# Batch 1's q and k loaded by four heads, early constant products and a new order of steps in a fused attention and gMLP kernel

## The chip, the cores and the metric

The kernel runs on one core of one Trainium2 chip. The metric is the device time of one execution in microseconds. The kernel before took 168.78 us, the median of three runs (167.84 to 169.89).

## What is computed

Two blocks follow each other: sliding-window attention with four sink positions, and a gMLP block on its output. Cut to what matters:

```python
# attention: batch 4, 8 heads, 768 positions, head size 64; n_sink 4, window 128
scores = (q @ k.transpose(0, 1, 3, 2)) / 8
keep = (pos[None, :] < 4) | ((rel >= 0) & (rel < 128))      # rel = row - column
a = softmax(where(keep, scores, -1e9))
x = (a @ v)                       # heads side by side: (4, 768, 512)
# gMLP: d_model 512, d_ff 1024
h = gelu_tanh(x @ w_in)           # (4, 768, 1024)
u, v = h[..., :512], h[..., 512:]
v_n = (v - mean(v)) / sqrt(var(v) + 1e-6) * g_ln
v_s = einsum('ts,bsd->btd', w_sg, v_n) + b_sg[None, :, None]
out = x + (u * v_s) @ w_out
```

All inputs and the output are float32 in HBM; the products are computed in bfloat16.

## The kernel before

The kernel is one long list of steps, STEPS (line 20). Each word of it names a function and its indices, and a loop at the end (line 615) calls them in this order. Inside an engine the order of the list is the order of execution; engines, and the two DMA queues (the software queue, issued by POOL, and SyncE's, SP), run past each other as far as semaphores between producer and consumer allow. Nothing else plans the work: what stands behind a waiting instruction on its engine waits too.

Indices: b is the batch (0 to 3), p a pair of heads (0 to 3), g a pair of 128-row blocks (0 to 2), t or j a block of 128 rows (0 to 5), hf a half of the 768 rows, dc a block of 128 of the 512 gate columns. A last letter names the engine: D is VectorE (DVE), A is ScalarE (ACT), P is GpSimd (POOL).

The steps of a batch, in the order of its data:

- LQ, LK (line 219, 222; the load itself is `load`, line 210) bring q and k as bfloat16 through the software queue; LFQ (line 225) brings the first four blocks of batch 0's q as float32 through SP; LV and LVH (line 231, 241) bring v. LW, LWS, LWO (line 246 to 255) bring the two halves of w_in, the two halves of w_sg and w_out, all through the software queue. LC and LG (line 258, 262) bring the sink rows of v, g_ln and b_sg (the tile b_bc) through SP.
- q and k are needed with the head dimension on the partitions. HOW (line 15) gives the way for each batch: "B" turns a loaded block with TensorE (TQ, TK through `turns`, line 320; eight transposes of 128 columns into one PSUM tile for two row blocks), and EQ, EK (`turned`, line 364) copy the result out of PSUM; "C" turns by a DMA transpose on SP (DQ, DK, `by_dma`). FTQ and FEQ do the same for LFQ's blocks.
- QK (line 428) makes the scores of a head pair and row pair, EX (line 441) takes their exponent on ACT into a tile P, MK (line 445) sets what lies outside the window to zero, on DVE by a product with a mask or on POOL by two affine selects. Where a QK step carries a last index 1, the mask is added on TensorE instead, by a product with a bias tile. KS, SK and SX do the sink columns.
- AV (line 467) multiplies P with v, NR (line 491) divides by the sum into x_sb. XT and XE (or the DMA transpose XD) turn x.
- MV and GV make the gate half of h (TensorE, then gelu on ACT), BN, RS, NM its mean and variance, Z the normalised half. MU and GU make the other half, already turned. WT and WE turn w_sg once, in batch 0. SP (a step, line 579) is the product with w_sg, GT and GM (line 586, 591) add b_sg and multiply with u, GM on DVE or POOL; OU (line 595) is the product with w_out, RA (line 602) adds x, ST stores.

PSUM holds two rings: two score tiles (sc) for QK, MV and MU, and four smaller ones (mm) for all else. A step that takes a tile waits until the step that read it last is done. k16, q16, kT and qT have two tiles each, so batch 2 takes those of batch 0.

HM n (line 179) asks that the next step that takes a PSUM tile first runs n products of constants into it (`fresh`, line 182), which its own products then overwrite. The list before has no HM.

Of the kernel before, what the change touches and what calls it, by code (L numbers as in the profile page):

```python
# [9 lines left out]
BF16 = mybir.dt.bfloat16  # L10
# [1 line left out]
ALU = mybir.AluOpType  # L12

PARTS = (0,)
HOW = "BBCC"
VHOW = "THHH"
BIG = 1e9


STEPS = """  # L20
LFQ.0 LK.0.0 LFQ.1 LFQ.2 LK.0.1 LFQ.3 LK.0.2 IDEN LK.0.3 IDEN2 FTQ.0 FILL LQ.0.4 FEQ.0.A FTQ.1 LQ.0.5 LC FTQ.2 MASK
FEQ.1.A LK.0.4 MASK0 TK.0.0 LK.0.5 FTQ.3 EK.0.0.A ZERO LG LV.0.0 QK.0.0.0 KS.0 FEQ.2.D QK.0.1.0.1 EX.0.0.0 LV.0.1
EX.0.1.0 TK.0.1 LV.0.2 QK.0.2.0 FEQ.3.A QK.0.3.0.1 VSK EX.0.2.0 LV.0.3 VSO EK.0.1.D TQ.0.2 EX.0.3.0 MK.0.0.0.D LV.0.4
QK.0.0.1 EQ.0.2.D QK.0.1.1 EX.0.0.1 LV.0.5 VSM.0 TK.0.2 EX.0.1.1 MK.0.2.0.D LW.0 QK.0.2.1.1 EK.0.2.D MK.0.0.1.P
QK.0.3.1.1 EX.0.2.1 SK.0.1 EX.0.3.1 LK.1.0 MK.0.1.1.D QK.0.0.2 AV.0.0.0 AV.0.1.0 LWS.0 AV.0.2.0 NR.0.0.0 SX.0.1
QK.0.1.2.1 EX.0.0.2 NR.0.1.0 LW.1 SK.0.2 NR.0.2.0 EX.0.1.2 AV.0.3.0 AV.0.0.1 MK.0.0.2.P NR.0.3.0 AV.0.1.1 SX.0.2
NR.0.0.1 QK.0.2.2 QK.0.3.2 LK.1.1 EX.0.2.2 NR.0.1.1 AV.0.2.1 AV.0.3.1 NR.0.2.1 AV.0.0.2 EX.0.3.2 MK.0.2.2.P XT.0.0
NR.0.3.1 AV.0.1.2 NR.0.0.2 XE.0.0.A XT.0.1 LQ.1.0 MK.0.3.2.D AV.0.2.2 XE.0.1.A NR.0.1.2 LQ.1.1 AV.0.3.2 MV.0.0
NR.0.2.2 LQ.1.2 NR.0.3.2 LWS.1 XT.0.2 GV.0.0 LK.1.2 MV.0.1 XE.0.2.D BN.0.0 LK.1.3 LQ.1.3 WT.0 GV.0.1 MV.0.2 LQ.2.0
BN.0.1 LQ.2.1 WT.1 GV.0.2 WT.2 LQ.1.4 MU.0.0 BN.0.2 RS.0.1 LQ.1.5 TQ.1.0 GU.0.0 MU.0.1 RS.0.2 WE.0.A WE.1.D WE.2.D  # L30
LK.1.4 NM.0.1 NM.0.2 Z.0.0.D Z.0.1.A MU.0.2 Z.0.4.D LK.2.0 GU.0.1 EQ.1.0.D LK.2.1 Z.0.2.A Z.0.3.D Z.0.5.D TK.1.0
LK.1.5 GU.0.2 SP.0.0.0 EK.1.0.D LVH.1.0 QK.1.0.0 GT.0.0.0 QK.1.1.0 WT.3 TQ.1.1 EX.1.0.0 WE.3.D LVH.1.1 SP.0.0.1 VSM.1
EX.1.1.0 EQ.1.1.D WT.4 DQ.2.0 LK.2.2 QK.1.2.0 KS.1 WE.4.A GT.0.0.1 QK.1.3.0 TK.1.1 MK.1.0.0.D LK.2.3 EX.1.2.0 WT.5
EK.1.1.D SP.0.0.2 EX.1.3.0 LWO WE.5.A QK.1.0.1 LK.2.4 GT.0.0.2 QK.1.1.1 TQ.1.2 EX.1.0.1 MK.1.1.0.D LQ.2.2 SP.0.1.0
EQ.1.2.D EX.1.1.1 MK.1.3.0.D LQ.2.3 DK.2.0 SK.1.0 MK.1.0.1.D QK.1.2.1 SX.1.0 LQ.2.4 QK.1.3.1 GM.0.0.0.D TK.1.2
# [39 lines left out]
def kernel(  # L75
# [14 lines left out]
    nc = tc.nc  # L90
# [16 lines left out]
    sb = ctx.enter_context(tc.tile_pool(name="sb", bufs=1))  # L107
# [22 lines left out]
    mm_ring = Ring("mm", 4, [128, 512], F32, psum)  # L130
# [21 lines left out]
    c16 = Ring("c16", 6, [128, d_model], BF16)  # L152
    iden = sb.tile([128, 128], BF16, name="iden")
    iden32 = sb.tile([128, 128], F32, name="iden32")
    mask0 = sb.tile([128, 512], BF16, name="mask0")
    mask1 = sb.tile([128, 512], BF16, name="mask1")
    bias0 = sb.tile([128, 512], BF16, name="bias0")
    bias1 = sb.tile([128, 512], BF16, name="bias1")
# [23 lines left out]
    def fresh(ring, key):  # L182
        t = ring.new(key)
        for _ in range(pre[0]):
            nc.tensor.matmul(t if ring is mm_ring else t[:, 0, :], iden, bias1, start=True, stop=True)
        pre[0] = 0
        return t

# [18 lines left out]
    def plain(ring, b, t):  # L207
        return ring.get((b, t // 3)).bitcast(F32)[:, d_model * (t % 3):d_model * (t % 3 + 1)]

    def load(ring, src, b, i):  # L210
        if HOW[b] in "FD":
            return nc.sync.dma_start(out=plain(ring, b, i).rearrange("p (h d) -> p h d", h=H), in_=heads(src, b, i))
        if HOW[b] == "A":
            dst = ring.get(b)[:, NH * HP * i:NH * HP * (i + 1)].rearrange("p (h f) -> p h f", h=HP)
# [49 lines left out]
        return nc.sync.dma_start(out=b_bc, in_=moe_b_sg.partition_broadcast(128))  # L264

    def IDEN():
        make_identity(nc, iden32)
# [385 lines left out]
```

## Time and profile before

| | before |
|---|---|
| median of three runs | 168.78 us |
| the profiled execution's own time | 168.27 us |
| its span, first to last instruction | 166.5 us |
| busy: ACT, POOL | 96.7, 105.8 us |
| HBM read, written | 24.81 MB, 6.29 MB |
| issues of q, k loads by POOL | 44, 0.91 to 0.93 us each |

PE is TensorE's products, PEld its weight loads. Engines work beside each other, so shares do not add up to one; what counts in a stretch is the engine, queue or wait that ends last there. The share of a DMA queue is the time that its packets took, summed over 16 engines; packets of one engine overlap, so it can be above 100%. A time line row gives start, length, engine, line, operation, the tiles written and read, and, in brackets, how long the engine was idle before and what ended it. The time to landing is counted from the issue's start.

### The profile page before, as it was taken

The numbers are of one execution on the slowest core, as the hardware profiler recorded it, in microseconds if no ns is written. First come the engines' busy times: TensorE is split into PE (matmuls) and PEld (weight loads), VectorE is DVE, ScalarE is ACT, GpSimd is POOL, SyncE is SP. The second block draws the span as 40 slices with busy tenths as digits, with TensorE's granted clock in tenths as the row PEclk, the third lists the DMA queues.
The fourth block names the chain that finished last, engine by engine and source line by source line (L and its number), as shares of the span: only waits on it lengthen the run. The fifth ranks groups of instructions, "written<-read, shape, count | busy, mean of one in ns | idle before, by whom it ended". The sixth has DMA issues, their size and how long they took to land.

```text
span 166.5 us, 3659 instructions
## 1 busy us (share of the span) xinstructions
PE 146.5 (88%) x1448; PEld 94.2 (57%) x1458; DVE 123.1 (74%) x289; ACT 96.7 (58%) x107; POOL 105.8 (64%) x131
## 2 busy tenths in 40 slices
PE   0598899997799767979999999999999999899990
PEld 0455467595566445744666675458656744585540
DVE  0346487775859999756976989859989964885881
ACT  3249789468659464297799660856988003683000
POOL 7997969599996399997807994907025930034220
PEclk9999999999789999999999999999999999999999
DMA  5999999999999999999999988999900436510055
GB/s 117 172 165 200 126 174 206 171 189 158 148 132 140 166 177 160 111 158 161 149 107 154 128 251 204 180 186 206 209 32 0 88 74 217 192 69 0 0 193 186
DMA packets 100321, 24.39 MB, mean 146 GB/s; under 512 B 94800, under 2 KB 97104, under 8 KB 100304
## 3 DMA queue, kind: packets, MB, share of 16 engines
q0 software_dynamic: 72912, 11.67, 102.4%
q1 hardware_dynamic: 27392, 12.49, 37.3%
q8 instruction: 11, 0.18, 0.4%
q14 instruction: 6, 0.05, 0.1%
HBM read 24.81 MB, written 6.29 MB: 187 GB/s over the span
## 4 chain that ended last, share of the span: by engine, by line
PE 43%; DVE 19%; DMA 12%; POOL 10%; ACT 7%; issue 6%; another core or an unknown queue 0%; ACTq 0%; DVEq 0%; POOLq 0%
PE mm L599 12%; PE mm L582 11%; DMA w_in_sb<-in_moe_w_in_dram 7%; PE sc L521 6%; PE sc L562 5%; DMA k<-in_k_dram 5%; DVE gtmp L587 4%; DVE P L450 4%; POOL q L217 4%; PE sc L438 3%; POOL k L217 3%; DVE wsg_gated L592 2%; ACT vt L525 2%; DVE x_sb L496 2%; DVE st L534 2%
## 5 line engine op out<-in xcount | busy, mean ns | idle before, releaser
L443 ACT ACTIVATE P<-sc 128x1024 bf16<-128x1024 f32 (+1 forms) x48 | 43.2, 956 | 14.6 <-PE sc L438 14.5
L582 PE MATMUL mm<-wsgT,z 128*128 128x384 bf16 x192 | 35.8, 333 | 3.8 <-DVE z L555 1.5
L582 PEld LDWEIGHTS <-z 128*128 128x128 bf16 x192 | 18.1, 99 | 16.3 <-issue 3.6
L592 POOL TENSOR_TENSOR wsg_gated<-gtmp,uT 128x384 bf16<-128x384 bf16 x18 | 16.9, 949 | 14.7 <-DVE gtmp L587 11.0
L587 DVE SCALAR_TENSOR_TENSOR gtmp<-mm,g_sb,b_bc 128x384 bf16<-128x384 f32 x32 | 19.2, 611 | 6.1 <-PE mm L582 6.0
L521 PE MATMUL sc<-w_in_sb,xT 128*128 128x512 bf16 x92 | 21.9, 379 | 2.0 <-ACT xT L194 1.0
L534 DVE BATCH_NORM_STATS2 st<-vt 128x6 f32<-128x512 f32 x24 | 15.4, 684 | 10.7 <-ACT vt L525 10.7
L217 POOL DMA_DIRECT2D k<-in_k_dram x24 | 22.2, 931 | 1.1 <-POOLq L636 0.8
L599 PE MATMUL mm<-w_out_sb,wsg_gated 128*128 128x512 bf16 x91 | 21.8, 379 | 0.3
L217 POOL DMA_DIRECT2D q<-in_q_dram x20 | 18.0, 909 | 6.4 <-PE sc L438 2.8
L562 PE MATMUL sc<-xT,w_in_sb 128*128 128x256 bf16 x192 | 21.9, 273 | 0.0
L562 PEld LDWEIGHTS <-w_in_sb 128*128 128x128 bf16 x192 | 18.6, 98 | 2.8
L496 DVE TENSOR_TENSOR x_sb<-mm,rcp 128x384 bf16<-128x384 f32 (+1 forms) x36 | 18.5, 513 | 1.2
L450 DVE TENSOR_TENSOR P<-P,mask 128x768 bf16<-128x768 bf16 (+1 forms) x26 | 18.8, 731 | 0.6 <-ACT P L443 0.6
L543 POOL TENSOR_TENSOR rs<-rs,neg_half 128x4 f32<-128x4 f32 (+1 forms) x8 | 7.3, 913 | 18.6 <-DVE rs L538 17.9
L453 POOL TENSOR_SCALAR_AFFINE_SELECT P<-P 128x512 bf16<-128x512 bf16 x17 | 11.5, 678 | 10.8 <-ACT P L443 10.7
L603 DVE TENSOR_TENSOR ot<-mm,x_sb 128x512 f32<-128x512 f32 x24 | 15.8, 684 | 3.4 <-PE mm L599 3.4
L479 PE MATMUL mm<-v_sb,P 128*128 128x65 bf16 x192 | 16.6, 194 | 1.2 <-DVE gtmp L587 0.8
L438 PE MATMUL sc<-qT,kT 64*128 64x128 bf16 (+1 forms) x256 | 15.4, 241 | 1.1 <-ACT P L443 0.6
L525 ACT ACTIVATE vt<-sc 128x1024 f32<-128x1024 f32 x12 | 12.2, 1024 | 7.0 <-PE sc L521 6.1
L521 PEld LDWEIGHTS <-xT 128*128 128x128 bf16 x96 | 9.1, 98 | 12.5 <-ACT xT L194 1.3
L483 PE MATMUL mm<-v_sb,P 128*128 128x65 bf16 x160 | 15.7, 194 | 0.4 <-POOL P L456 0.4
(75 smaller groups left out, 226.8 us busy)
## 6 DMA issues: line engine op xcount, KB each, us to landing
out_dram<-ot SPq DMA_DIRECT2D x24, 256.0 KB, 3.0
k<-in_k_dram POOLq DMA_DIRECT2D x24, 128.0 KB, 7.3
q<-in_q_dram POOLq DMA_DIRECT2D x20, 128.0 KB, 8.3
v_sb<-in_v_dram POOLq DMA_DIRECT2D x6, 384.0 KB, 9.5
wsg_gated<-in_moe_w_sg_dram POOLq DMA_DIRECT2D x2, 576.0 KB, 10.6
ot<-in_q_dram SPq DMA_DIRECT2D x4, 256.0 KB, 5.1
w_in_sb<-in_moe_w_in_dram POOLq DMA_DIRECT2D x2, 512.0 KB, 11.2
v_sb<-in_v_dram POOLq DMA_DIRECT2D x6, 128.0 KB, 9.5
```

Of the source, the lines that this page charges most:

```text
L217: return nc.gpsimd.dma_start(out=dst.rearrange("p (h d) -> p h d", h=H), in_=heads(src, b, i))
L438: nc.tensor.matmul(sc[:, hl, c:c + 128 * ni], at(kT, b)[rows, j, p, :], at(qT, b)[rows, i:i + ni, p, :], start=not biased, stop=(not biase ...
L443: nc.scalar.activation(out=P.new((b, p, g))[:, :, 0:w], in_=sc_ring[b, p, g][:, :, 0:w], func=AF.Exp, scale=scale)
L450: nc.vector.tensor_mul(pt[:, :, 0:w], pt[:, :, 0:w], m.unsqueeze(1).to_broadcast([128, 2, w]))
L496: nc.vector.tensor_mul(x_sb.get(b)[:, i0:i0 + n, 128 * p:128 * (p + 1)].rearrange("p t (h d) -> p t h d", h=2), av[:, :, :, 0:Dh], rcp[:, ...
L521: nc.tensor.matmul(hp[:, jl, :], xT[b][:, 2 * g + jl, c, :], w_in_sb[:, c, d_half:2 * d_half], start=(c == 0), stop=(c == KD - 1))
L534: nc.vector.bn_stats(out=sts[jl], in_=vt[b, g][:, jl, :])
L562: nc.tensor.matmul(hp[:, dc // 2, 256 * (dc % 2):256 * (dc % 2 + 1)], w_in_sb[:, c, 128 * dc:128 * (dc + 1)], xT[b][:, 2 * g:2 * g + 2, c, :],
L582: nc.tensor.matmul(ps[:, 0:NH], z[b][:, si, 128 * dc:128 * (dc + 1)], wsgT[:, si, NH * hf:NH * (hf + 1)], start=(si == 0), stop=(si == NT ...
L587: nc.vector.scalar_tensor_tensor(out=gtmp.new((b, hf, dc)), in0=mm_ring["g", b, hf, dc][:, 0:NH], scalar=g_sb[:, dc:dc + 1], in1=b_bc[:, N ...
L592: (nc.vector if e == "D" else nc.gpsimd).tensor_mul(gated(b, hf)[:, dc, :], gtmp[b, hf, dc], uT[b][:, dc, NH * hf:NH * (hf + 1)])
L599: nc.tensor.matmul(ps, gated(b, hf)[:, dc, 128 * tl:128 * (tl + 1)], w_out_sb[:, dc, :], start=(dc == 0), stop=(dc == KU - 1))
```

## The change

Four things change. HOW becomes "BACC": batch 1's q and k are loaded in the way "A", which is in the code of both kernels: a load takes four heads with all 768 rows, partition p gets rows 6p to 6p + 5 of each head, a run of 1.5 KB in HBM in place of 256 bytes, and there are four such loads (LQ.1.0, LQ.1.1, LK.1.0, LK.1.1) in place of twelve. TQ.1 and TK.1 then turn a pair of heads g (0 to 3) with all its rows, by twelve transposes of 64 columns, two side by side in the partitions of one PSUM tile; EQ.1 and EK.1 copy 768 columns out and put the rows back in order, reading PSUM with a stride. A tile `warm` of zeros is set by DVE in the first step (WARM), the constant products read it in place of iden and bias1, and three HM steps ask for 6 + 2 + 2 of them. And the whole list of steps is in a new order, with other engines for some of them: XE four times on DVE for ACT, WE twice; MK on POOL 23 times for 17; GM on POOL 12 times for 18.

```diff
-HOW = "BBCC"
+HOW = "BACC"
 STEPS = """
-LFQ.0 LK.0.0 LFQ.1 LFQ.2 LK.0.1 LFQ.3 LK.0.2 IDEN LK.0.3 IDEN2 FTQ.0 FILL LQ.0.4 FEQ.0.A FTQ.1 LQ.0.5 LC FTQ.2 MASK
...
+WARM LFQ.0 IDEN LFQ.1 LK.0.0 LFQ.2 IDEN2 FILL LFQ.3 LK.0.1 LK.0.2 HM.6 FTQ.0 LC LK.0.3 FTQ.1 MASK LQ.0.4 MASK0 HM.2
+FTQ.2 VSK LQ.0.5 VSO FEQ.0.D FEQ.1.A FTQ.3 FEQ.2.A LK.0.4 TK.0.0 FEQ.3.A LK.0.5 EK.0.0.D LV.0.0 ZERO HM.2 QK.0.0.0
+QK.0.1.0.1 EX.0.0.0 LV.0.1 VSM.0 TK.0.1 EX.0.1.0 LV.0.2 QK.0.2.0 EK.0.1.D EX.0.2.0 QK.0.3.0.1 KS.0 LV.0.3 MK.0.0.0.D
+TQ.0.2 EX.0.3.0 MK.0.2.0.D QK.0.0.1 LQ.1.0 EQ.0.2.D EX.0.0.1 QK.0.1.1.1 LV.0.4 SK.0.1 EX.0.1.1 TK.0.2 LV.0.5
+QK.0.2.1.1 EK.0.2.D SX.0.1 MK.0.0.1.P AV.0.0.0 EX.0.2.1 AV.0.1.0 AV.0.2.0 NR.0.0.0 QK.0.3.1.1 LW.0 NR.0.1.0 SK.0.2
+EX.0.3.1 NR.0.2.0 LK.1.0 QK.0.0.2 AV.0.3.0 AV.0.0.1 LK.1.1 NR.0.3.0 SX.0.2 AV.0.1.1 EX.0.0.2 AV.0.2.1 NR.0.0.1
+QK.0.1.2 NR.0.1.1 XT.0.0 MK.0.0.2.P EX.0.1.2 AV.0.3.1 XE.0.0.D QK.0.2.2 QK.0.3.2 NR.0.2.1 MK.0.1.2.P EX.0.2.2 TQ.1.0
+NR.0.3.1 AV.0.0.2 EQ.1.0.A MK.0.2.2.P TQ.1.1 NR.0.0.2 EX.0.3.2 XT.0.1 AV.0.1.2 LK.2.0 XE.0.1.A AV.0.2.2 MK.0.3.2.D
+MV.0.0 LK.2.1 EQ.1.1.D LW.1 NR.0.1.2 AV.0.3.2 NR.0.2.2 LWS.0 GV.0.0 MV.0.1 NR.0.3.2 LWS.1 BN.0.0 LQ.1.1 XT.0.2 GV.0.1
+LQ.2.0 TK.1.0 XE.0.2.D TK.1.1 LQ.2.1 EK.1.0.D TK.1.2 DK.2.0 TK.1.3 LK.2.2 BN.0.1 QK.1.0.0 MV.0.2 EX.1.0.0 LG EK.1.1.D
+RS.0.1 MU.0.0 GV.0.2 LQ.2.2 NM.0.1 Z.0.0.A Z.0.1.D LQ.2.3 BN.0.2 MU.0.1 GU.0.0 LVH.1.0 EK.1.2.D EK.1.3.A WT.0 GU.0.1
+WT.1 WE.0.D MU.0.2 RS.0.2 WE.1.D Z.0.2.A NM.0.2 Z.0.4.A Z.0.5.D KS.1 LK.2.3 MK.1.0.0.D WT.2 GU.0.2 WT.3 WE.2.D WT.4
+WT.5 WE.3.D WE.4.A QK.1.1.0 WE.5.D QK.1.0.1 LVH.1.1 TQ.1.2 Z.0.3.D TQ.1.3 EQ.1.2.D SP.0.0.0 EX.1.1.0 LWO DQ.2.0
...
+GM.0.0.3.P QK.1.3.2 EX.1.3.1 SP.0.1.2 NR.1.0.1 MK.1.2.2.P MK.1.3.0.D EX.1.3.2 SP.0.1.3 NR.1.1.0 MK.1.3.1.P
+GT.0.1.2 QK.2.0.0 QK.2.1.0 EX.2.0.0 GT.0.1.3 AV.1.2.0 MK.1.3.2.P AV.1.3.0 EX.2.1.0 AV.1.1.1 MK.2.0.0.D NR.1.2.0
+AV.1.2.1 GM.0.1.2.P QK.2.2.0 NR.1.3.0 QK.2.3.0 EX.2.2.0 LK.2.4 AV.1.3.1 NR.1.1.1 OU.0.0 EX.2.3.0 LQ.3.0 NR.1.2.1
+XT.1.0 LVH.2.0 NR.1.3.1 QK.2.0.1 DQ.2.2 QK.2.1.1 EX.2.0.1 XE.1.0.D OU.0.1 RA.0.0 LK.3.0 EX.2.1.1 XT.1.1 GM.0.1.3.D
+XT.1.2 GM.0.1.1.D LK.2.5 MV.1.0 RA.0.1 LVH.2.1 KS.2 XE.1.1.D XE.1.2.D MV.1.1 GV.1.0 MK.2.1.1.P BN.1.0 LQ.3.1 MV.1.2
...
+MK.3.1.2.P SP.2.0.2 GT.2.0.0 GT.2.0.1 AV.3.1.1 GM.2.0.0.D GT.2.0.2 GM.2.0.1.P AV.3.2.1
+NR.3.1.1 AV.3.3.1 OU.2.3 NR.3.2.1 NR.3.3.1 OU.2.4 RA.2.3 XD.3.1 OU.2.5 RA.2.4 SP.2.0.3 GM.2.0.2.D ST.2.3 ST.2.4 MV.3.0
+GT.2.0.3 GM.2.0.3.D OU.2.0 GV.3.0 OU.2.1 RA.2.0 MV.3.1 ST.2.0 RA.2.1 RA.2.5 ST.2.1 BN.3.0 ST.2.5 MV.3.2 ST.1.5 GV.3.1
+BN.3.1 OU.2.2 GV.3.2 MU.3.2 BN.3.2 RS.3.1 MU.3.0 GU.3.2 RA.2.2 RS.3.2 NM.3.1 NM.3.2 Z.3.0.A Z.3.1.D MU.3.1 Z.3.2.D
...
+    warm = sb.tile([128, 512], BF16, name="warm")
...
-            nc.tensor.matmul(t if ring is mm_ring else t[:, 0, :], iden, bias1, start=True, stop=True)
+            nc.tensor.matmul(t if ring is mm_ring else t[:, 0, :], warm[:, 0:128], warm, start=True, stop=True)
...
+    def WARM():
+        nc.vector.memset(warm, 0.0)
```

In the list before, three LK.0 loads stand ahead of IDEN, LG (with b_sg) stands ahead of LV.0.0, LK.1.0 is the only load of batch 1 or 2 ahead of w_in's second half (LW.1), half of w_sg (LWS.0) stands ahead of it, and WT.3 to WT.5, TQ.1.1 to TK.1.2 and all of QK.1 stand behind SP.0.0.0.

## The prediction

> **What bounds the kernel now.** I read the page first, then busy time by stretches, then the waits and the time line inside the stretch that loses most. Page and stretches (columns: stretch, length, then busy time of PE, PEld, DVE, ACT and POOL with instruction counts, granted clock, DMA share, GB/s):
>
> ```profile
> PE 146.5 (88%) x1448; PEld 94.2 (57%) x1458; DVE 123.1 (74%) x289; ACT 96.7 (58%) x107; POOL 105.8 (64%) x131
> q0 software_dynamic: 72912, 11.67, 102.4%
> ```
>
> ```profile
> 0.00:27.00 27.00, 19.08 (x247) 13.11 (x249) 13.86 (x49) 16.42 (x21) 23.16 (x37) 1.00 1.96 162
> 27.00:40.20 13.20, 12.97 (x120) 9.47 (x118) 8.41 (x26) 8.65 (x10) 10.84 (x13) 1.00 1.83 180
> 40.20:67.80 27.60, 22.43 (x285) 14.82 (x286) 24.70 (x44) 17.59 (x21) 23.15 (x29) 0.94 2.10 154
> 67.80:106.50 38.70, 37.41 (x369) 23.04 (x371) 31.12 (x74) 27.68 (x30) 29.20 (x34) 1.00 1.59 158
> 106.50:137.80 31.30, 30.71 (x294) 19.68 (x296) 26.55 (x61) 16.94 (x18) 13.95 (x16) 1.00 0.89 121
> 137.80:163.20 25.40, 23.90 (x145) 14.09 (x144) 18.40 (x41) 9.43 (x10) 5.46 (x6) 1.00 0.32 117
> ```
>
> The cuts are at first products: MV.0.0, SP.0.0.0, MV.1.0, MV.2.0, MV.3.0. From 67.8 on PE is the bound (37.4 of 38.7, 30.7 of 31.3, 23.9 of 25.4). In 40.2 to 67.8 it is not: DVE is busy 24.7 of 27.6. Up to 40 the loads decide: w_in's first half is issued at 16.64 and lands 9.9 later, at 26.5, and MV.0.0 starts at 27.1. The software queue delivers in the order of issue and always owes something: its small q loads, issued 0.87 apart, land 0.84 apart.
>
> DVE is not slow by its own work only. In the time line:
>
> ```profile
> 59.04 2.60 DVE L592 TENSOR_TENSOR wsg_gated<-gtmp,uT 128x384 bf16<-128x384 bf16 x1
> 59.62 0.63 POOL L453 TENSOR_SCALAR_AFFINE_SELECT P<-P 128x512 bf16<-128x512 bf16 x1
> 60.21 0.63 POOL L456 TENSOR_SCALAR_AFFINE_SELECT P<-P 128x512 bf16<-128x512 bf16 x1
> 60.80 0.63 POOL L453 TENSOR_SCALAR_AFFINE_SELECT P<-P 128x512 bf16<-128x512 bf16 x1
> ```
>
> That product has a median of 0.357 us; it stood still for 2.2 us while POOL ran selects back to back.
>
> The last stage has one hole:
>
> ```profile
> 140.00 1.28 ACT L525 ACT_TABLE_LOAD   x1 [10.83 <-PE sc L521]
> 142.37 1.89 PE L521 MATMUL sc<-w_in_sb,xT 128*128 128x512 bf16 x8 [0.72 <-ACT vt L525]
> ```
>
> MV.3.2 waits for a score buffer that GV.3.0 holds, which waits for its table: some 1.2 us with nothing between.
>
> **Prices, from unstalled rows.** PE: MV 1.73 (eight products, 29.27 to 31.00), MU 1.74 (33.73 to 35.48), SP 0.98 (eight in 7.80 at the end), OU 0.87, eight transposes 0.44 (35.48 to 35.92), WT 0.35, QK 0.16 or 0.21, AV 0.36 to 0.6. DVE: GT 0.60, GM 0.36, NR 0.18 + 0.56, MK 0.55 or 0.68, RA 0.69, BN 1.5 to 1.7, WE 0.55, XE 0.69, Z 0.54. Multiplied with the counts of both lists of steps, PE has 134 us either way, DVE 125 either way. POOL loses 61 − 53 issues (−8 small ones at 0.92 = −7 us), gets six mask pairs more (23 for 17, 1.27 each) and six gate products fewer (12 for 18, 0.95): −5 us in all. ACT loses four XE and two WE, wins two Z, and has two table loads more (12 for 10).
>
> **The parts.**
>
> Loads. Twelve loads of 256 KB read become four of 786 KB. Small ones take 0.84 us of queue, so 10.1. No row has this shape; by bytes, half of w_sg (1.18 MB read in 3 KB runs) takes 2.8, so 786 KB takes 1.9. Ends: w_in's first half at its fastest (1.05 MB in 1.75) gives 1.3; no gain at all gives 2.5. I take 1.9 as the nearest row: 7.6 in place of 10.1.
>
> Order of that queue. Moved past it: LQ.1.0 now stands ahead of LV.0.4, LK.1.0, LK.1.1, LK.2.0, LK.2.1 ahead of w_in's second half, and that ahead of both halves of w_sg. Before, LV.0.5 landed at 14.79 + 10.0 = 24.8. After it lands at about 26.0: one big load ahead (+1.9), against which b_bc (384 KB, in flight 9.4 to 16.2) is gone from this time (−0.7). Then w_in 27.8 (+1.75), LK.1.0 and LK.1.1 31.6, two small 33.3, LW.1 35.9 (+2.6; it was 20.39 + 12.4 = 32.8), LWS.0 38.7, LWS.1 41.6 (39.0 before), LQ.1.1 43.5. The weights come some 3 us later. PE's order puts work there: from MV.0.0 to SP.0.0.0 it has 15.8 us (MV 5.2, MU 5.2, six WT 2.1, six turns 2.0, rest 1.3) against 12.7. So MV.0.0 at 27.8, MU.0.0 about 36, SP.0.0.0 at 44.0 instead of 40.25, with 103.2 us of PE work left instead of 106.5. Up to here it is a draw, and there is no cover: each microsecond of a later weight is one of PE's.
>
> Turns. Ninety-six transposes of 64 columns for forty-eight of 128. The trace has products into 32 columns (L417): four of 512 columns take 0.40 us together, one takes 0.389, so column groups overlap. By that row twelve turns take 0.33, serially 0.64 (12 × 0.44/8): 0 to +2.5 us in all; I take 0.5. The copies out read PSUM with a stride: 768 elements take 0.55 by WE's row, or 0.95 at the rate of the f32 copy (512 in 0.69). I take 0.95; two of them, +0.8, fall into the stretch where DVE is full.
>
> The Trainium skill, TensorEngine Tiling (Array Packing), Restrictions and Gotchas, speaks against this part: column tiling excludes the fast weight load, and changing the mode drains the array. The trace's 32-column loads take 92 ns and the full ones 98, so it shows no loss there; by the rule the turns would cost the serial end, 2 us more.
>
> Warm products. The memset of warm (row of mask: 0.49) ends at about 1.3; six products of 512 columns, at twice the warm pitch of 0.22, end by 4.0, and the first q block lands at about 4.1. The identity is made before the first k load and not after three, which takes away the 4.8 us that PE waits for it, and puts 0.5 us ahead of LK.0.0. TK.0.0 needs LK.0.1, so QK.0.0.0 stays at 11.3. Faster products (the bias pair 0.82 at 11.71, 0.50 at 13.91) gain 0.5 us there; then w_in's landing takes it all back. Worth nothing; without the cover at most 1 us either way.
>
> The stretch from SP.0.0.0 to MV.1.0. PE has 17.8 us in both. DVE had 20.7 by prices and was held 4 more; after it has 18.5 + 0.4, since the EK, WE and most EQ are already done, and I leave 3 us for standing behind POOL (the clock, granted at 0.94 here, I leave as it is). 44.0 + 22 = 66.0 for MV.1.0 instead of 67.9, though OU.0.0, OU.0.1 and two XT more are already done.
>
> From MV.1.0. PE has 85.3 us left instead of 88.7. Stage by stage, with the losses of before: to SP.1.0.0 14.5 + 1.6 gives 82; to MV.2.0 DVE leads, 16.9 + 1, gives 100; to MV.3.0 29.0 + 1.7. Here a new wait comes: between AV.2.3.1 and MV.2.1 PE now has 5.3 us (three OU, four QK, SK, MV.2.0) where it had 7.9, while NR.2.3.1 ends 2.5 us after the AV and XD took 4.7 to land: 7.2 − 5.3 = 1.9 late. That gives 132.6. To the end 26.0 + 0.8 (the hole before MV.3.2 now holds OU.2.0 to OU.2.2; OU.2.3 to OU.2.5, SP.2.0.3 and MV.3.0 cover XD.3.1) gives 159.4. The span ended 3.3 us after the last DVE step, and the execution is 168.27 against a span of 166.5, 1.8 around it: 159.4 + 3.3 + 1.8 = **164.5**. The median of the runs is 168.78, 0.5 above the profiled one; I leave that as scatter.
>
> **Rivals.**
>
> Weights late (**167.5**, chance 0.16). If a four-head load takes 2.5, three of them stand ahead of LWS.1: +1.8 at SP.0.0.0; LWO, behind the same queue, then holds OU.0.0, ahead of XT.1.0, for another microsecond: 164.5 + 3. For it: the chain of before already has w_in's DMA with 7%. Against: runs of 2 and 3 KB move faster in the same queue.
>
> POOL's selects hold DVE (**172**, chance 0.24), the one that ends slower. Six pairs more stand on POOL, three in a row twice, and DVE has twenty gate products for fourteen, all between PE and the gated buffers that OU needs. If each of six runs costs the 2.2 us of the row above, DVE loses 13 where I left 5: 164.5 + 8. It decides beyond four such stalls. Against: masks on DVE fall from 26 to 20. The Trainium skill, SBUF — State Buffer, SBUF: two separate sides, calls this an exclusive lock held for one instruction; by that each stall would be one select, 0.63, and this rival would vanish; the row shows four.
>
> The parts don't do what they say (**165.5**, chance 0.12): the turns run serially, +2, half of it before SP.0.0.0 where PE has just enough time, half where it waits for copies anyway.
>
> My forecast has 0.48. Faster by over 1%: 0.48 + 0.12 = 0.60, same 0.16, slower 0.24; 1% is about what a measurement of this kernel tells from no change. The range goes from 160 (three loads at 1.3 ahead of LWS.1, −1.8; copies at 0.55, −0.8; no wait at MV.2.1, −1.9) to 172.
>
> **What would show it.** LWS.1 landing near 41.6 and LQ.1 loads 1.9 us apart; SP.0.0.0 near 44; MV.1.0 near 66; a PE wait before MV.2.1 of some 2 us; no hole before MV.3.2; L592 on DVE with few instances above 1 us. Wrong if PE waits for a DMA anywhere between 28 and 44 us for more than 2 us, or if the stretch from SP.0.0.0 to MV.1.0 is again near 27 us.

## The result, and the profile after

The changed kernel takes **170.63 us** (median of 20 runs, 169.10 to 173.77), the kernel before 168.43 on the same chip (20 runs, 167.07 to 170.65). The ratio is 1.012, with a 95% interval of 1.009 to 1.015: slower by over 1%, where I had forecast 164.5 and a gain. The time lies inside my range of 160 to 172, on the wrong side.

The profile taken with the result is of a disturbed execution (span 172.1), so the lines below are of a second profile of the same kernel, "again" (171.23 us, span 169.5). From its page, busy time and the software queue:

```profile
PE 150.9 (89%) x1516; PEld 96.4 (57%) x1516; DVE 131.3 (77%) x295; ACT 96.8 (57%) x106; POOL 99.2 (59%) x129
q0 software_dynamic: 62544, 11.67, 87.7%
```

The change does to the queue what it says: 10,400 packets fewer for the same 11.67 MB, and 87.7% in place of 102.4%. Yet PE is busy 4.4 us longer. The stretches, cut at the same first products as before (MV.0.0, SP.0.0.0, MV.1.0, MV.2.0, MV.3.0), tell where:

```profile
0.00:29.09 29.09, 23.65 (x274) 15.19 (x275) 15.64 (x52) 16.37 (x20) 25.46 (x41) 0.89 1.59 159
29.09:46.84 17.75, 16.91 (x218) 12.56 (x215) 14.76 (x36) 15.43 (x18) 10.52 (x12) 0.98 1.42 180
46.84:74.77 27.93, 21.79 (x269) 14.42 (x266) 22.69 (x40) 15.09 (x18) 22.75 (x28) 0.88 2.07 136
74.77:108.61 33.84, 32.50 (x333) 19.99 (x331) 30.41 (x66) 25.37 (x28) 23.16 (x30) 1.00 1.39 151
108.61:139.02 30.41, 29.70 (x279) 19.02 (x278) 26.46 (x59) 15.78 (x17) 13.80 (x17) 1.00 0.95 127
139.02:164.90 25.88, 25.88 (x158) 15.26 (x156) 20.36 (x46) 8.72 (x9) 3.53 (x4) 1.00 0.38 105
```

The third stretch was to shrink from 27.6 to 22 us and is 27.9, with DVE no longer its bound (22.7 of 27.9) and the clock at 0.88. The waits of "again" between 50 and 70 us name the cause (columns: sum, times, longest):

```profile
PEld L483 <- DMA v_sb<-in_v_dram: 5.6, 2, 4.8
PE mm L483 <- DMA v_sb<-in_v_dram: 5.0, 2, 4.5
```

PE's time line there, POOL's at the issue of that load, and PE in the stretches behind the wait:

```profile
61.37 0.51 PE L442 MATMUL sc<-qT,kT 64*128 64x256 bf16 x8
66.40 0.35 PE L483 MATMUL mm<-v_sb,P 128*128 128x65 bf16 x3 [4.53 <-DMA v_sb<-in_v_dram]
```

```profile
46.29 1.42 POOL L243 DMA_DIRECT2D v_sb<-in_v_dram  x1 [1.95 <-DMA q<-in_q_dram]
```

```profile
66.00:68.00 2.00, 1.60 (x27) 1.60 (x28) 0.69 (x3) 0.00 (x0) 2.00 (x3) 0.50 1.12 58
68.00:70.00 2.00, 2.00 (x33) 1.80 (x32) 1.57 (x6) 0.00 (x0) 2.00 (x3) 0.50 1.86 139
70.00:72.00 2.00, 2.00 (x28) 1.23 (x25) 1.32 (x4) 1.54 (x2) 1.64 (x2) 0.85 2.62 151
72.00:75.00 3.00, 3.00 (x42) 2.22 (x41) 2.48 (x7) 1.95 (x3) 0.00 (x0) 1.00 2.45 159
```

AV.1.2.0 is the first product that reads heads 4 to 7 of v of batch 1, and their load, LVH.1.1, lands at 66.4. It was issued only at 46.29, because POOL first waited 1.95 us for a q load (LQ.1.1, landed at 46.0). While it waited, eight transfers of this queue were in flight, LQ.1.1 the oldest. From issue to landing it took 20.1 us. PE stood still for 4.8 us, and for 4 us behind that it was busy at half its clock. Where before PE waited for DVE, it now waits for a load.

### The profile page after: what moved, and what is told of

It reads as the page before. It is cut to its first block, busy times and chain, and to the rows that moved or that the text cites. A ratio compares the mean times of both kernels' runs of the same rounds, so it can differ in the third digit from the quotient of the medians.

```text
span 172.1 us, 3783 instructions
## 1 busy us (share of the span) xinstructions
PE 150.1 (87%) x1503; PEld 95.3 (55%) x1516; DVE 131.3 (76%) x295; ACT 97.0 (56%) x106; POOL 99.2 (58%) x129
## 3 DMA queue, kind: packets, MB, share of 16 engines
q0 software_dynamic: 62544, 11.67, 85.4%
## 4 chain that ended last, share of the span: by engine, by line
PE 45%; DMA 28%; DVE 12%; POOL 4%; ACT 4%; issue 3%; SPq 1%; DVEq 0%; ACTq 0%
DMA v_sb<-in_v_dram 12%; PE mm L586 10%; PE mm L603 9%; DMA q<-in_q_dram 9%; PE sc L525 8%; DMA ot<-in_q_dram 5%; PE sc L566 4%; PE sc L442 4%; DMA out_dram<-ot 2%; DVE P L454 2%; DVE st L538 2%; PE mm L483 2%; DVE wsg_gated L596 2%; DVE gtmp L591 2%; DVE ot L607 1%
## 5 line engine op out<-in xcount | busy, mean ns | idle before, releaser
L447 ACT ACTIVATE P<-sc 128x1024 bf16<-128x1024 f32 (+1 forms) x48 | 43.8, 953 | 24.0 <-PE sc L442 22.8
L586 PE MATMUL mm<-wsgT,z 128*128 128x384 bf16 x192 | 34.1, 327 | 0.2 <-DVE gtmp L591 0.2
L483 PE MATMUL mm<-v_sb,P 128*128 128x65 bf16 x192 | 18.1, 203 | 8.5 <-DMA v_sb<-in_v_dram 5.8
L586 PEld LDWEIGHTS <-z 128*128 128x128 bf16 x192 | 18.1, 98 | 12.6 <-issue 0.7
L457 POOL TENSOR_SCALAR_AFFINE_SELECT P<-P 128x512 bf16<-128x512 bf16 x23 | 15.7, 681 | 15.6 <-ACT P L447 11.2
L603 PE MATMUL mm<-w_out_sb,wsg_gated 128*128 128x512 bf16 x88 | 22.9, 383 | 0.5
L483 PEld LDWEIGHTS <-P 128*128 128x128 bf16 x192 | 15.7, 103 | 10.0 <-DMA v_sb<-in_v_dram 6.1
L596 POOL TENSOR_TENSOR wsg_gated<-gtmp,uT 128x384 bf16<-128x384 bf16 x12 | 11.3, 947 | 15.5 <-DVE gtmp L591 10.9
L607 DVE TENSOR_TENSOR ot<-mm,x_sb 128x512 f32<-128x512 f32 x24 | 16.2, 685 | 3.1 <-PE mm L603 2.6
L547 POOL TENSOR_TENSOR rs<-rs,neg_half 128x4 f32<-128x4 f32 (+1 forms) x8 | 7.0, 872 | 19.8 <-DVE rs L542 19.8
L487 PE MATMUL mm<-v_sb,P 128*128 128x65 bf16 x160 | 17.2, 202 | 0.0
L218 POOL DMA_DIRECT2D k<-in_k_dram x18 | 16.3, 918 | 0.9 <-DMA wsg_gated<-in_moe_w_sg_dram 0.7
L460 POOL TENSOR_SCALAR_AFFINE_SELECT P<-P 128x512 bf16<-128x512 bf16 x23 | 16.6, 721 | 0.0
L454 DVE TENSOR_TENSOR P<-P,mask 128x768 bf16<-128x768 bf16 (+1 forms) x20 | 15.3, 768 | 0.4 <-ACT P L447 0.4
```

The source lines that it names most:

```text
L447: nc.scalar.activation(out=P.new((b, p, g))[:, :, 0:w], in_=sc_ring[b, p, g][:, :, 0:w], func=AF.Exp, scale=scale)
L454: nc.vector.tensor_mul(pt[:, :, 0:w], pt[:, :, 0:w], m.unsqueeze(1).to_broadcast([128, 2, w]))
L483: nc.tensor.matmul(av[:, il, hl, :], pt[:, hl, c:c + 128], vb[:, h, i, :], start=first, stop=False)
L586: nc.tensor.matmul(ps[:, 0:NH], z[b][:, si, 128 * dc:128 * (dc + 1)], wsgT[:, si, NH * hf:NH * (hf + 1)], start=(si == 0), stop=(si == NT ...
L603: nc.tensor.matmul(ps, gated(b, hf)[:, dc, 128 * tl:128 * (tl + 1)], w_out_sb[:, dc, :], start=(dc == 0), stop=(dc == KU - 1))
L607: nc.vector.tensor_add(ot.new((b, t)), mm_ring["o", b, t], x_sb[b][:, t, :])
```

## The experiments

Each kernel is written as a change to a list of steps. All times are medians, the ratios are to the kernel before on the same chip, with 95% intervals.

**The changed kernel again, and its two suspects one by one.** "again" changes nothing.

> The changed kernel as it is, for its stages in an undisturbed execution. Both theories: 170.4 us, the start of MV.0.0 near 28, SP.0.0.0 near 47, a wait of PE for v before AV.1.2.0 of 3 to 5 us, and from MV.1.0 to the end some 92 us, as in the first profile of it (76.9 to 168.8). If the wait before AV.1.2.0 is missing here, it belongs to the disturbed execution and the theory below falls.

Measured: 170.66 us, 1.011 (1.002 to 1.019). In "zero_early" the four memsets of ZERO leave the place behind EK.0.0:

```diff
-... IDEN2 FILL LFQ.3
+... IDEN2 FILL ZERO LFQ.3
...
-EK.0.0.D LV.0.0 ZERO HM.2
+EK.0.0.D LV.0.0 HM.2
```

> ZERO (the memsets of v's ones columns) moved from behind EK.0.0 to behind FILL; nothing else. Theory A (the start is lost to this step: on POOL LV.0.1 waits 4.2 us for it and all later loads stand behind): LV.0.1 to LV.0.5 and LQ.1.0 are issued 4 us earlier, w_in lands 1 to 2 us earlier, 169 us. Rival B (the software queue is full anyway, and POOL next waits for EX.0.0.1): loads are issued earlier, w_in's second half and w_sg land as before within 0.5 us, 170.4.

Measured: 170.14 us, 1.009 (1.005 to 1.014). In "again" the wait is there, on POOL:

```profile
12.76 0.88 POOL L234 DMA_DIRECT2D v_sb<-in_v_dram  x1 [1.89 <-DVE ks_sink L311]
```

It holds every later issue by 1.9 us, but taking it away gives 0.5 us that the intervals don't separate from nothing. In "v_early" the two v loads leave the places behind the rows of batch 2:

```diff
-LQ.2.0 TK.1.0 XE.0.2.D TK.1.1 LQ.2.1 EK.1.0.D
+LQ.2.0 TK.1.0 XE.0.2.D TK.1.1 LQ.2.1 LVH.1.0 LVH.1.1 EK.1.0.D
...
-GU.0.0 LVH.1.0 EK.1.2.D
+GU.0.0 EK.1.2.D
...
-QK.1.0.1 LVH.1.1 TQ.1.2
+QK.1.0.1 TQ.1.2
```

> LVH.1.0 and LVH.1.1 (batch 1's v) moved ahead of LK.2.2, LQ.2.2, LQ.2.3 and LK.2.3 in POOL's order; nothing else. Theory A (5.1 us of the loss are PE waiting for the second half of batch 1's v, which stands behind batch 2's loads): v lands near 58 to 60 instead of 67.8, the wait before AV.1.2.0 is gone, 166.5 us. Rival B (DVE and ACT are as late, or QK.2.0.1 now waits for the delayed q and k of batch 2): the wait moves elsewhere, 169 to 171.

Measured: 168.09 us, 1.001 (0.996 to 1.005). The wait at AV.1.2.0 falls from 4.8 to 0.2 us, the stretch from SP.0.0.0 (48.87) to MV.1.0 (71.24) from 27.9 to 22.4. But SP.0.0.0 itself came 2 us later than in "again": something is given back ahead of it. "three" is both moves, and TK.0.0 ahead of FTQ.3 as in the kernel before:

```diff
-FTQ.3 FEQ.2.A LK.0.4 TK.0.0 FEQ.3.A
+TK.0.0 FTQ.3 FEQ.2.A LK.0.4 FEQ.3.A
```

> Both moves, and TK.0.0 ahead of FTQ.3 as in the kernel before, so that the first scores don't wait for the fourth block of q (it landed at 11.8). Theory A: QK.0.0.0 at 11.5 instead of 13.5, MV.0.0 near 27, SP.0.0.0 near 45.5, no wait for v: 163 to 165. Rival B: the gains don't add, since the same loads end the stretch up to SP.0.0.0: 166 to 168.

Measured: 167.31 us, 0.997 (0.993 to 1.001). What was given back stands in the time lines of "three", POOL's first:

```profile
37.03 0.88 POOL L218 DMA_DIRECT2D k<-in_k_dram  x1 [1.18 <-DMA w_in_sb<-in_moe_w_in_dram]
37.93 1.06 POOL L547 TENSOR_TENSOR rs<-rs,neg_half 128x4 f32<-128x4 f32 x1
40.10 0.93 POOL L218 DMA_DIRECT2D q<-in_q_dram  x1 [1.11 <-DMA wsg_gated<-in_moe_w_sg_dram]
43.50 0.87 POOL L218 DMA_DIRECT2D q<-in_q_dram  x1 [2.47 <-DMA wsg_gated<-in_moe_w_sg_dram]
44.39 0.73 POOL L547 TENSOR_TENSOR rs<-rs,neg_half 128x2 f32<-128x2 f32 x1
```

then ACT's:

```profile
45.40 0.81 ACT L556 ACTIVATE z<-vt,nmr,rs 128x512 bf16<-128x512 f32 x1 [2.09 <-DVE nmr L550]
46.12 1.00 ACT L571 ACTIVATE uT<-sc 128x1024 bf16<-128x1024 f32 x1
```

and two of its stretches:

```profile
45.00:47.50 2.50, 0.32 (x6) 0.22 (x5) 2.32 (x7) 2.10 (x3) 1.04 (x2) 1.00 1.49 202
47.50:50.00 2.50, 2.50 (x33) 1.56 (x31) 1.70 (x4) 2.47 (x4) 1.49 (x2) 0.66 2.46 157
```

L547 (RS) is a layer-norm step on four numbers a row. It is POOL's, and POOL takes its work in order: RS.0.1 and RS.0.2 stand behind loads that wait for an older transfer to land (each time the eighth before it in the queue). RS.0.2 comes at 44.39; NM, Z.0.4 and GU.0.2 follow one after another; QK.1.0.1 needs the score buffer that GU.0.2 empties; PE does 0.32 us of work in 2.5, and then goes on at a clock of 0.66.

**Taking the layer-norm steps out from behind the loads.** "rs_free" is "three" with

```diff
-LK.2.2 BN.0.1 QK.1.0.0 ... RS.0.1 ... LQ.2.2 ... LQ.2.3 ... RS.0.2
+BN.0.1 RS.0.1 QK.1.0.0 ... RS.0.2 LK.2.2 LQ.2.2 LQ.2.3
```

> As three (ZERO behind FILL, TK.0.0 ahead of FTQ.3, LVH.1.0 and LVH.1.1 behind LQ.2.1), and RS.0.1 put right behind BN.0.1, LK.2.2, LQ.2.2, LQ.2.3 behind RS.0.2, so that on POOL no layer-norm step stands behind a load that waits for a place in the queue. Theory: in three this wait ran on through RS.0.2, NM.0.2, Z.0.4 and GU.0.2 to a 2.5 us stall of PE at QK.1.0.1 and a clock of 0.66 to 0.83; without it RS.0.1 comes at 36, RS.0.2 at 41.5 to 42, QK.1.0.1 waits under 0.5 us, SP.0.0.0 starts at 46.5 to 47.5 (TQ.1.2 still waits for LQ.1.1 at 46), 165.5 to 166.8 us. Rival: SP.0.0.0 is held by the weights and LQ.1.1 anyway: 167.3 +- 0.5 us as three.

Measured: 166.03 us, 0.990 (0.983 to 0.997). RS.0.2 ran at 38.0, QK.1.0.1's wait was gone, SP.0.0.0 started at 44.45. The same kernel once more:

> rs_free unchanged, with more rounds, as the measure beside rs_no_warm and q_first on the same chip. 166.0 +- 0.6 us, ratio to before 0.985 to 0.992.

Measured: 166.45 us, 0.991 (0.987 to 0.995). This order is faster than both kernels. Its third stretch is 23.1 us long, with DVE as the bound that I had forecast (22.55 of it):

```profile
45.41:68.47 23.06, 20.25 (x269) 13.19 (x267) 22.55 (x41) 14.47 (x18) 21.39 (x27) 1.00 2.08 154
```

**Two attempts at more.** "four" and "q_first" pull LQ.1.1 and the weights forward, by pushing back two k rows of batch 2 in "rs_free":

```diff
-LK.2.0 ... LK.2.1 ... LW.1 ... LQ.1.1
+LW.1 ... LQ.1.1 LK.2.0 LK.2.1
```

is "four", which also has LG right behind LC, and

```diff
-LK.2.0 ... LK.2.1 ... LW.1 ... LQ.1.1 ... DK.2.0 ... RS.0.1
+LW.1 ... LQ.1.1 ... RS.0.1 LK.2.0 LK.2.1 DK.2.0
```

is "q_first", which also has LG ahead of LQ.2.0.

> As rs_free, and LK.2.0, LK.2.1 behind LQ.1.1 in POOL's queue, the layer-norm and gate biases (LG) loaded right behind LC. Theory: the second half of w_in then lands at about 35 us (36.7 in three), the last gate weights at 41.5 (43.2) and LQ.1.1 at 44 to 44.5 (46.1); MU.0.0 doesn't wait, SP.0.0.0 starts at 45 to 46 and MV.1.0 at 67.5 to 68.5, 164 to 165.5 us. Rival: what is pushed back (the k rows of batch 2, and so the DMA transpose DK.2.0) lands late and batch 2's first scores wait: 166 to 168 us.

> rs_free, and LK.2.0, LK.2.1 moved from ahead of LW.1 to behind RS.0.1, DK.2.0 behind them, LG ahead of LQ.2.0. Theory: the weights and LQ.1.1 land 1.6 us earlier (LQ.1.1 at 42, the second half of v at 52.5), TQ.1.2 waits 0 in place of 1.3 us, no load ahead of RS.0.1 waits for a place in the queue: SP.0.0.0 at 43 to 43.5, 164.5 to 165.5 us. Rival: as in four, an issue ahead of RS.0.1 has to wait for the eighth transfer before it and holds RS.0.1: SP.0.0.0 at 45 or later, 166.5 to 168.5 us.

Measured: "four" 168.24 us, 1.005 (1.000 to 1.010); "q_first" 168.68, 0.998 (0.991 to 1.005). Both lost the gain. LQ.1.1 did land early, at 41.7 and 42.4. In "four" the v loads now stood behind eight others, and RS.0.1 behind them:

```profile
34.31 1.41 POOL L243 DMA_DIRECT2D v_sb<-in_v_dram  x1 [1.01 <-DMA w_in_sb<-in_moe_w_in_dram]
37.48 1.41 POOL L243 DMA_DIRECT2D v_sb<-in_v_dram  x1 [1.75 <-DMA wsg_gated<-in_moe_w_sg_dram]
38.90 1.05 POOL L547 TENSOR_TENSOR rs<-rs,neg_half 128x4 f32<-128x4 f32 x1
```

so SP.0.0.0 came at 47.18, 2.7 later than in "rs_free": about its rival's time, by another cause. In "q_first" SP.0.0.0 came at 44.51, 0.9 ahead of "rs_again", and the stretch behind it took 27.8 us. Its profile (of an execution of 170.3 us, 1.6 above the median) has POOL waiting 2.6 and 1.9 us for a place in the queue, DVE 2.3 us for a gate product behind these on POOL, and a clock of 0.53 to 0.62 from 56 to 64 us. No run shows that these belong together, and the median runs may not have them, so why "q_first" lost the gain stays open. In both, b_sg's load, now issued at 8 us, ran beside the first v loads; LV.0.0 landed at 17.8 and 18.2, against 16.1 in "rs_free" and 17.2 in "rs_again".

**The loads and turns alone.** "loads_only" is the kernel before with the layout of batch 1 changed, and only what follows from that moved:

```diff
-HOW = "BBCC"
+HOW = "BACC"
...
-LK.1.0 ... LW.1 ... LK.1.1 ... LQ.1.0 ... LQ.1.1 ... LQ.1.2 ... LWS.1 ... LK.1.2 LK.1.3 LQ.1.3 LQ.1.4 LQ.1.5 LK.1.4 LK.1.5
+LW.1 ... LQ.1.0 ... LK.1.0 ... LWS.1 LQ.1.1 ... LK.1.1
```

> Before, with its order of steps, and of the change only the loads of batch 1 by four heads and their turns by 64 columns (loads of batch 1 put at LQ.1.0, LK.1.0, then behind LWS.1: LQ.1.1, LK.1.1; each pair turned ahead of its first scores; KS.1 behind the last EK.1). Theory: the loads and turns themselves cost nothing, the loss comes from the new order of the queue: 166 to 169 us, LVH.1.1 landed by 56 us as in before, no wait for it. Rival: the form itself costs (64-column turns, all four pairs needed before the first third's scores): 170 us or more, with the stretch from the first gate product SP.0.0.0 to MV.1.0 longer than the 27.6 us of before.

Measured: 170.93 us, 1.020 (1.013 to 1.028). The number is the rival's, the mechanism is not: SP.0.0.0 came at 39.61 (before 40.25), and then PE waited 3.25 us at AV.1.2.0 for LVH.1.1, in flight from 39.7 to 61.5 beside two transposes by DMA. "loads_v" moves only LVH.1.0 and LVH.1.1, to right behind LK.1.1:

> loads_only with LVH.1.0 and LVH.1.1 right behind LK.1.1 in the queue. Theory: in loads_only the loads by four heads and the turns gained 0.6 us up to SP.0.0.0 and 1.4 us up to the arrival at AV.1.2.0 against before, and then lost 3.25 us there to LVH.1.1, which was in flight from 39.7 to 61.5 us beside DMA transposes; ahead of the rows of batch 2 it lands by 51 us and the wait is gone: 166.5 to 168 us. Rival: the form itself costs, in the stage behind as well: 170 us or more.

Measured: 167.26 us, 0.991 (0.987 to 0.996). LVH.1.1 landed at 49.45 and AV.1.2.0 waited 0.1 us. So the loads by four heads with their turns, and with the places that the loads have in this list, are worth close to 1%, once the v load isn't made to pay for them; what of it is the form alone, no run separates.

**The late v load alone.** "v_late" is the kernel before with one step moved:

```diff
-LVH.1.1 SP.0.0.1 VSM.1 ... LQ.2.3 DK.2.0
+SP.0.0.1 VSM.1 ... LQ.2.3 LVH.1.1 DK.2.0
```

> Before, with one step moved: LVH.1.1 (second half of v of batch 1) from its place at the first gate products to behind LQ.2.3 in POOL's queue, behind eight loads of batch 2 and of w_out. Theory: this place alone makes the loss of the changed kernel. The transfers ahead of it landed at 64 us in before; it lands at 62 to 65 us, PE waits 3 to 5 us at AV.1.2.0 (no wait in before), 171 to 173 us. Rival: before has enough other work behind AV.1.2.0 in its order and on DVE to take the wait up: under 169.5 us.

Measured: 173.90 us, 1.041 (1.036 to 1.046). The loads between its old place and its new one are six, not eight. It landed at 66.5, and PE waited for it twice as long as I expected:

```profile
PEld L479 <- DMA v_sb<-in_v_dram: 10.1, 1, 10.1
```

```profile
57.00:66.50 9.50, 0.00 (x0) 0.00 (x0) 1.75 (x4) 1.33 (x2) 7.83 (x12) 0.64 2.18 157
66.50:70.00 3.50, 3.46 (x33) 2.45 (x34) 2.28 (x6) 0.00 (x0) 0.00 (x0) 0.51 1.54 147
```

PE came to AV.1.2.0 3 us earlier than in the kernel before (56.4 for 59.6); so of 10 us of wait 6.4 reach the time (173.90 against 167.48 on that chip). The second stretch shows again what follows such a gap: 3.5 us at half the clock.

**The new order of the later stages alone.** "splice" has the steps of "loads_v" up to MV.1.0, and what is left in the order of the changed kernel.

> The steps of loads_v up to MV.1.0, and from there those that are left, in the order of the changed kernel. Theory: the new order of the later stages is worth about 3 us (from MV.1.0 to the end of OU.3.5 the profiles show 90.6 us in rs_again and 93.9 in loads_v), and the loads and turns of batch 1 are worth 1 us ahead of it: 163 to 165 us. Rival: what is shorter behind MV.1.0 in the changed order is only work that it does ahead of MV.1.0: 166 to 167.5 us as loads_v and rs_free.

Measured: 169.15 us, 1.013 (1.008 to 1.018); its profiled execution took 166.89. The forecast of 163 to 165 is refuted; why the median is above the profile is open. The nearest comparison is with "loads_v", which has the same PE steps on either side of AV.1.2.0: from there to the last OU.3.5 its profile takes 100.9 us (59.46 to 160.40) and that of "splice" 99.9 (60.56 to 160.50), so the later order gave 1.0 us of the 3 expected. The same stretch in before and then in "v_early":

```profile
59.64:161.98 102.34, 97.25 (x907) 61.16 (x912) 83.02 (x187) 58.31 (x62) 56.73 (x67) 1.00 1.11 135
```

```profile
63.99:161.80 97.81, 94.92 (x886) 59.49 (x883) 84.86 (x187) 54.62 (x58) 50.44 (x61) 1.00 1.00 131
```

It is 4.5 us shorter. 2.3 of these are busy time of PE (97.25 against 94.92), for the most part work that the changed order has done ahead of AV.1.2.0 (AV.1.0.1, QK.2.0.0, QK.2.1.0, SP.0.1.3), and 2.2 are idle time that is gone (5.1 against 2.9).

**The constant products.** "no_warm" is the changed kernel without WARM and the HM steps, "rs_no_warm" is "rs_free" without them.

> The changed kernel without its constant products (the memset of warm and the HM steps are gone; the one place that is left is none). Theory: they buy nothing, because before ran its first stage at a granted clock of 1.00 without them, and the undisturbed profile of the changed kernel shows 0.83 at 7.5 to 10 us and 0.50 at 10 to 12.5 us with them. Time 170.6 +- 0.7 us, first masked score QK.0.0.0 at 11.2 to 12 us. Rival: they hold the clock up and without them the first stage runs longer: 171.5 to 172.5 us.

> rs_free without its constant products (the memset of warm and the HM steps are gone). Theory: no_warm was 2.6 us over the changed kernel because the products do help: with them the 32-bit turns FTQ.3 took 0.41 us in rs_free, without them 0.72 us in before and no_warm, both at a granted clock of 1.00; so 167.3 to 168.8 us, FTQ.3 at 0.7 us again, QK.0.0.0 at 11 to 11.5. Rival: no_warm was hit by the landing of its fourth q block alone (11.04 against 9.49 us in again), which TK.0.0 ahead of FTQ.3 now takes off the chain: 165.6 to 166.6 us.

> The changed kernel itself once more, as the measure beside no_warm_again on the same chip: 170.4 +- 0.6 us.

> no_warm once more. In rs_free the constant products bought nothing (166.64 without against 166.45 us with them), in the changed kernel 2.6 us. Theory: with FTQ.3 ahead of TK.0.0 the first stage of the changed kernel hangs on the fourth q block, ZERO and through them on POOL's queue, and the constant products shorten that chain: 172.3 to 173.6 us, QK.0.0.0 at 13 us or later. Rival: the four runs of no_warm were disturbed: 170 to 171 us.

Measured: "no_warm" 173.26 us, 1.035 (1.027 to 1.042); "rs_no_warm" 166.64, 0.989 (0.985 to 0.993), beside 166.45 with them; then, on one chip, "after_again" 171.46, 1.024 (1.019 to 1.028), and "no_warm_again" 169.41, 1.014 (1.010 to 1.019). By the ratios to before, the same kernel without the products was 2.3% slower than with them (1.035 on one chip against 1.011 of "again" on another), and 0.9% faster side by side; the side-by-side runs count for more, and in "rs_free" the products buy nothing. Why the four runs of "no_warm" took so long is open; in their profile the fourth q block landed at 11.0 and QK.0.0.0 came at 13.8 (12.6 in "no_warm_again"). The rows of the clock (the column after POOL), in "after_again", then in "no_warm_again":

```profile
7.50:10.00 2.50, 0.74 (x5) 0.45 (x5) 0.75 (x3) 0.58 (x1) 2.50 (x4) 0.72 1.99 186
10.00:12.50 2.50, 2.50 (x14) 1.82 (x14) 0.53 (x1) 0.58 (x1) 0.86 (x1) 0.50 2.35 156
```

```profile
7.50:10.00 2.50, 1.30 (x5) 0.91 (x6) 0.76 (x3) 0.58 (x1) 2.50 (x4) 1.00 2.00 181
10.00:12.50 2.50, 1.78 (x12) 1.45 (x11) 0.68 (x1) 0.58 (x1) 0.88 (x2) 1.00 2.35 156
```

The 1.00 of "no_warm_again" is not full speed. Its trace has no record of the clock ahead of 18.3 us, and a row reads 1.00 where there is none; the record starts at 12 to 20 us in the kernels without constant products, before among them, and at 4 to 7 us in those with them. The products' own times tell the speed. The same pair of bias products in "after_again", then in "no_warm_again":

```profile
15.62 0.50 PE L437 MATMUL sc<-bias,iden 128*128 128x384 bf16 x2
15.59 0.82 PE L436 MATMUL sc<-bias,iden 128*128 128x384 bf16 x2
```

In before that pair takes 0.82 us at 11.71 and 0.50 at 13.91, and the record starts at 13.3. So without constant products PE is slow up to the start of the record, and my expectations for "no_warm" and "rs_no_warm", which took the 1.00 for the clock, rest on a wrong reading. The products do bring full speed earlier: the four 32-bit transposes FTQ.2 take 0.71 us in "after_again" (at 8.13) and 1.12 in "no_warm_again" (at 7.77). Then PE slackens while it waits for q, and in all profiles of kernels with them, except those of "rs_free" and "four", the clock falls back to 0.50 for 3.4 to 6.8 us.

## Why the prediction was wrong

The sum, by its own landmarks ("again" against the forecast): MV.0.0 29.1 for 27.8, +1.3; from there to SP.0.0.0 17.75 for 16.2, +1.5; to MV.1.0 27.9 for 22, **+5.9**; to MV.2.0 33.8 for 34, −0.2; to MV.3.0 30.4 for 32.6, −2.2; to the last step of DVE 27.0 for 26.8, +0.2. Unrounded they sum to 6.7, which leads from 164.5 to the 171.2 of that execution. Of the +1.3 at MV.0.0 little is the load that I let it wait for: w_in landed at 28.05, forecast for 27.8, and PE was still at earlier steps, at half its clock from 26.2 to 29.6.

**The step that failed** is "The stretch from SP.0.0.0 to MV.1.0 ... 44.0 + 22 = 66.0". It counts the work of PE and DVE and no load. My "Order of that queue" ended with LQ.1.1, and left out the steps behind it: LVH.1.0 among batch 2's q loads and LVH.1.1 behind them all, where before they stood ahead of these. LVH.1.1 was the transfer that I should have followed to its first reader, as I had done with w_in. "v_early" shows the stretch at 22.4 once that load is ahead, which gives back 2.6 us of the time (170.66 to 168.09 on one chip), and "v_late" that its place alone turns the kernel before into one of 173.9.

Two more terms of that order were missing. I let POOL issue its loads whenever it came to them; but an issue waits while eight transfers of its queue are in flight, and what is behind it on POOL, be it a layer-norm step, waits too ("three" against "rs_free": 0.7% of the time, some 1.2 us, with intervals that overlap a little; the stall of PE itself is gone from the trace). And the order of ZERO and TK.0.0 on DVE and PE held the first loads ("zero_early", and "three" against "v_early": 0.5 and 0.8 us, each no more than the scatter).

**Weights late** was right in part, by another cause than the one it named. With no transfer of SP beside it a four-head load costs what I took: LK.1.0 and LK.1.1 land 1.9 us apart in "again", 1.6 to 2.0 in most of the others (2.3 and 2.6 in "no_warm" and "no_warm_again"). The first one, LQ.1.0, landed 3.9 us after the load ahead of it in "again", and 1.7 in "zero_early", where no issue ahead of it waits for ZERO. Up to LW.1 the forecast order holds within 0.3 us (36.1 for 35.9). But LWS.1 landed at 43.1 for 41.6, and LQ.1.1 at 46.0 for 43.5, and SP.0.0.0 was 2.8 late. In these 9.9 us LWS.0, LWS.1 and LQ.1.1 took 3.8, 3.2 and 2.9, while the transpose DK.2.0 and b_sg's load were in flight; in "four", where b_sg had landed and no transpose was in flight yet, they took 2.8, 2.9 and 1.9. I had priced transfers one after another, in one queue; those that SP issues take their share.

**POOL's selects hold DVE** did not decide, though its 172 is the nearest number. In the third stretch DVE is busy 22.7 where it was 24.7. The stall itself is real; DVE in "again", beside POOL's selects:

```profile
50.63 2.63 DVE L318 TENSOR_TENSOR v_sink<-vs,headsel 128x512 bf16<-128x512 f32 x1
```

(0.69 at 12.85.) It falls on other steps; the twenty gate products have a mean of 0.53 us, where fourteen had 0.64.

**Right**: twelve turns of 64 columns overlap. Forty-eight took 1.53 us in "again", 0.38 for twelve:

```profile
33.76 1.53 PE L337 MATMUL mm<-iden,k 128*64 128x128 bf16 x48
```

where I had bounds of 0.33 and 0.64. All ninety-six took 3.8 us, +1.1 where I took +0.5: 0.53 and 0.85 for the first two groups of twelve, the second at half the clock, and 0.86 for the last two. The Trainium skill, TensorEngine Tiling (Array Packing), Restrictions and Gotchas, excludes the fast weight load under column tiling, for which I had priced the serial end, 0.64; no loss of that size shows at full clock. The copies took 0.95. The hole before MV.3.2 is gone. The warm products are worth nothing in "rs_free"; in the changed kernel the two measurements disagree. **Wrong on the good side**: no wait came before MV.2.1 (0.1 us), which is most of the −2.2.

With the missing steps put right, "rs_free" takes 166.0 and 166.5 us, 1.5 to 2 above the forecast; what is left is SP.0.0.0 at 44.5 to 45.4 for 44.0, and the third stretch at 23 to 24.3 for 22.

## What to carry to other kernels

When an order of steps is new, list for each load of a queue its place, and follow every one to its first reader, the ones that the change doesn't speak of first: a load that is only passed by others loses as much as one that is moved. On an engine that issues loads and also computes, look for what small step stands behind an issue that may have to wait for a place in the queue. And price a gap of PE with what follows it: here 3 to 4 us at half the clock behind gaps of 5 and 10 us.

## What the runs showed of the hardware

**An issue waits for the eighth load before it.** In all eighteen profiles here no load on POOL was issued while more than seven older ones of its queue were still to land, and the long waits at issues end when the eighth before has landed: LVH.1.1 for LQ.1.1 in "again", LK.2.2 for LW.1 and LQ.2.2 for LWS.0 in "three". The traces also name what is waited for: the loads of this queue use eight completion semaphores in turn (106 to 113 in "again"), and an issue waits for its own, whose last use is the load eight before. That is how this program deals out its semaphores; whether the queue itself would take more, no run shows.

**Transposes by DMA slow the software queue, and are slowed.** LVH.1.1 took 2.9 us of queue behind LVH.1.0 in "loads_v" (46.55 to 49.45), with none in flight, and 8.2 us behind LK.2.3 in "again" (58.19 to 66.36), with two issued ahead of it. Part of these 8.2 us went to the next load, w_out, whose packets ran between; by bytes the queue moved 0.45 MB in the 2.9 us and 0.72 MB in the 8.2, 155 and 88 GB/s. DK.2.0, 256 KB, was in flight for 12 us in "again". The Trainium skill, Advanced Engine Details and Errata, X-Bar Transpose (TRN2), has transposes as fast as plain DMAs, at 350 to 400 GB/s; by that it would take an estimated 0.7 us. No run here shows one alone; beside a full queue the rate was some 20 GB/s.

**The clock.** The Trainium skill, TensorE: Matmul & The Clock Gate, Why this matters for your kernels, asks for no idle gaps above some 3 us, since the array then goes back to half its clock. The gaps of 4.8 us in "again" and 10 us in "v_late" agree: 0.50 for 4 us, 0.51 for 3.5. But shorter ones did it too. In "again" PE was busy 0.58 of the microsecond from 24 and 0.12 of the next, and the clock was 0.61, 0.50, 0.50 and 0.68 in the four after these:

```profile
25.00:26.00 1.00, 0.12 (x4) 0.01 (x1) 0.00 (x0) 1.00 (x2) 1.00 (x3) 1.00 1.30 208
26.00:27.00 1.00, 1.00 (x17) 0.78 (x16) 0.61 (x3) 0.11 (x1) 1.00 (x2) 0.61 1.31 199
27.00:28.00 1.00, 1.00 (x13) 0.97 (x12) 1.00 (x3) 0.00 (x0) 1.00 (x2) 0.50 1.30 202
```

and no gap of PE was over 0.9 us there. Half speed stands in the record in stretches of 3.41 us or a multiple. Cut in step with them, the rows of "again" before and in this fall are:

```profile
22.81:26.22 3.41, 1.93 (x40) 1.35 (x37) 1.62 (x5) 3.09 (x4) 3.41 (x7) 1.00 1.27 192
26.22:29.64 3.42, 3.42 (x45) 2.94 (x43) 2.86 (x8) 1.52 (x2) 3.42 (x5) 0.50 1.49 194
```

So PE was busy 0.57 of the stretch ahead. With every profile cut in this way, a stretch at full speed with PE busy 0.42 or less was always followed by one at half, and one with 0.58 or more never; in between both occur, and what decides there stays open.
